# The stored order of a hand-scheduled recurrence and FFN kernel is searched anew

## The chip, the cores and the metric

The kernel runs on one core of one Trainium2 chip. The metric is the device time of one execution in microseconds (us). One core has TensorE (PE, matmuls, with its weight loads shown as PEld), VectorE (DVE), ScalarE (ACT), GpSimd (POOL) and SyncE (SP, which here issues the DMAs). PE writes to PSUM, which has eight banks of 512 fp32 columns on each partition.

## The reference, cut to what matters

```python
def _attn_ref(q, k, v, a_re, a_im):            # (4, 8, 768, 48) each
    mag = np.sqrt(a_re * a_re + a_im * a_im)
    scale = np.minimum(mag, 0.999) / (mag + 1e-06)
    a_re_n, a_im_n = (a_re * scale, a_im * scale)
    S_re, S_im = zeros((B, H, D, D)), zeros((B, H, D, D))
    for t in range(S):
        ar, ai = (a_re_n[:, :, t, :, None], a_im_n[:, :, t, :, None])
        new_re = ar * S_re - ai * S_im
        new_im = ar * S_im + ai * S_re
        kv = np.einsum('bhd,bhe->bhde', k[:, :, t], v[:, :, t])
        S_re, S_im = (new_re + kv, new_im)
        y[:, :, t] = np.einsum('bhd,bhde->bhe', q[:, :, t], S_re)
    return y

def _moe_ref(x, w_in, w_out):                  # (3072, 384), (384, 2048), (2048, 384)
    h = x @ w_in
    g = h * (1.0 / (1.0 + np.exp(-1.702 * h)))
    return g @ w_out

x = attn_out.transpose(0, 2, 1, 3).reshape(3072, 384)
out = _moe_ref(x, w_in, w_out)
```

A gated complex recurrence over 768 steps makes a 48-wide output for each of 4 × 8 heads. The 8 heads of a token stand side by side (384) and go through a two-layer feed-forward block of 2,048 hidden columns. The output of the kernel is written transposed.

## The kernel before, in words

**The recurrence** is computed in chunks. There are 12 units of 256 tokens, three for each batch, and each unit has two chunks of 128 tokens. `prepare(u)` loads the gate values (`ri`) and q and k (`qk`, L406); ACT takes logarithms, exponentials, arc tangents, sines and cosines of them, each of three table sets; DVE forms running sums along the tokens (`tensor_tensor_scan`) and the products that scale and rotate q and k (helper `both`, L276). Five DMAs of SP then move each result from (heads and dims) on partitions into `qkh`, where a head has its own columns (`remap`, L451 to L463). `attend(u)` works on the two chunks: scores on 32-column tiles of the PE array into `p_ps` (L498), times a mask on DVE (`pm`, L502), the mix with v and with the carried state into `x_ps` (L523), a copy to x on ACT (L533) or DVE (L534). For the state, k is turned by PE transposes of 112 × 112, two in one operation, into `k_ps` (L554), copied to `kt` by ACT (L557) or DVE (L558), and multiplied with v on tiles into `z_ps` (L548); DVE adds that to the state (L563, or L567 where the state is new).

**The feed-forward block** `moe(n)` runs for 7 blocks of tokens: units 0 and 1 alone (256 columns, weights and values as whole fp32, one matmul for each product), then five blocks of two units (512 columns, each value split in a high part and a rest, so three matmuls for each product). For each of 8 slices of 256 hidden columns, f = 0 and 1: H (L604) into `h_ps`, the activation G on ACT (L613 whole, L617 split), for the split blocks `gh` (rounded, L620 on ACT or L621 on DVE) and `gl` (the rest, L623 on DVE), then O (L637), which sums all slices into the three `o_ps`. At the end of a block the copies L652 or L653 and one output DMA (three for the last block).

**PSUM.** The eight banks are `p_ps`, `kz_ps` (both `k_ps` and `z_ps` are parts of it), `x_ps`, two `h_ps` and three `o_ps`. With 256 columns the two halves of one `h_ps` bank are used in turn: slice i of half f goes to half i % 2 of `h_ps[f]`.

**Weights** arrive as 64-bit numbers. `convert(n)` rebuilds fp32 from the two words (L294 loads, one of its DVE results is `valA`, L303); `split(n)` makes the rounded part (L312 on ACT, L313 on DVE) and the rest (L315) for the split blocks. `inspect` and `extent` look over all inputs for values outside the fast path's bounds, `decide` counts them, and `general()` would do the work again if any were found. Thirteen matmuls of no consequence (L445) go ahead of the first scores, into `h_ps[0]`.

**The order.** Nothing is issued while it is planned: each of these steps calls `plan.add`, which gives it the next number, the engine that it runs on, perhaps another engine that could do it, and the numbers of the steps that it depends on. Then `Plan.order` reads the stored string: every two bytes are the number of a step, and the steps of `OTHER` change to their second engine.

```python
def order(self):
    coded = base64.b85decode("".join(ORDER))
    order = struct.unpack(f">{len(coded) // 2}H", coded)
    place = {n: i for i, n in enumerate(order)}
    for n in OTHER:
        self.ops[n] = self.alt[n][:2] + self.ops[n][2:3] + self.alt[n][2:] + self.ops[n][4:]
    assert all(place[d] < place[n] for n, o in enumerate(self.ops) for d in o[4])
    return order

with tc.manual_schedule(engines={ENG.PE, ENG.Activation, ENG.DVE, ENG.Pool, ENG.SP}):
    for n in order:
        o = plan.ops[n]
        if o[5] not in (None, cur):
            nc.scalar.preload_act_table_set(o[5])
            cur = o[5]
        o[3]()
```

Each engine runs its own steps in the order of the string. A table of activation functions is loaded (shown at L836) wherever the next ACT step that needs one needs another than the current. What one step must wait for on another engine is enforced by semaphores.

Of the kernel before, what the change touches and what calls it, by code (L numbers as in the profile page):

```python
# [112 lines left out]
}  # L113
ORDER = (
    "08jvb0000A0Ac`<0J#7U08#)^08{`|0D}Nk0E7Ts09F8t0D%Bk0097i09pW800RLE09ybB09gQD0HXk10D=Hz0A>J%01E(L0A~P(0Am1P0EqyH0R"
    "jMN0Ez&J0AT=V0RsSy0R#YQ0Av9L0BZpT0Bit^0S5qW0F(g;0B!(|0B-=50B``00FnT40Sf?-0G0r901yCk0Db^;0GI%E0FwZj0CoVE00sbe00ID"
# [2 lines left out]
    "a<02Kf-0MG!`03-m{02Tlj044y^03`qz0M-E00UrP;0j&WU0NMa20U!X_04@O<05<_4051U>0LB0_0NVh`05AYF05t&00V4o00N?;N06_rZ04V@Q"
    "0Neo{0Nns80NDU50VDw;04xCJ0VM$)06YN80OJ7O0Ve^k0j>ci0Vn|90OA100Vx1N0OSF%0kHuq0ObHf0V)A30kQzh07n4q0kZ%-0WAQ{07L-i05"  # L120
    "||Y0PX-e07U@p06qb^0Qdnf0Pg@g0O$eo0O<fg0O|lq06PJ?0P6w50Pq2{0Pz900kr|Y0mA{f07wD0080Tl0lNVC0Ym{g0gVAV0Wbl?0XqS_0XzX"
    "Q0P+FG0WJZ(0X+de07?P&0Wtx;0P_Jq0mT6`0h<9p0QCXE0W<*g0mlI~0l)zE0YL%t0m=cR0Zjom0m%W&0muMM0Yw4K0XG570YU)x0Zsu%0Qvw;0"
    "Yd@K0Z#!(0Z;+-0aF3b0Z0K!0Q&(^08RnW0ZIT*0ZRe*0rdd<0a5|@0aO7@0Q~|00s8^c0r>%60sH~_0a^i*0+<2*0s#SF0gnOy0sR6A0a*cJ0bv"
    "3L0tx|Z0b2n60s;YC0aXFh0agK50iOY70n`EL0s{gI0o(!v0o4Hi0g(Y_0RRF80oDPj0RaJ*0u2HT0bK!(0tf+K0tW&P0b>FW0uch40uTZc0b~Jf"
    "0o?)>0-6DL0u%w60u}*h0-FLC0cZi<0cio>0gwS$0dWD60-OQS0pbFk0qFsh0pJ3j0uuq(0-pic0-*uf0;U3@0jmLQ0;B=s0qO#!0;2(P0-yq?0;"
    "~by0crxM0hI#l0ptPe0<QsX0dE0x0onnb0dN790doSd0qg;F0p$X*0d@ki0hj`*0owwq0eu0Q0<!|E0wMvN0p<c30p|i30<Hn=0<;0{0iFTx0_*~"
    "<0wV!_0e=E60__4C0eAtR0e}JU0eJ$p0we+(0wn_O0<{7r0eb=*0eS(U0w)5u0ek_X0=NRX0`UQa0r3H)0`CI50w@CX0xtsd0v!VN0v-Y%0=fZ#0"
    "`LO%0=xq90=)t$0fGWB0i*&d0`~$j0xJR_0{H?g0{8)^0yqJK0wDr91BL=J0xbeM0{a3p0fquJ0y_bP0yP3W0yY9Z0{Q`m0j2^!0yhFc0|Ehv0{;"
    "U10!0G-0jL850{#K20f_=c0jvT^0|W+L0g3{@0#5=;1BU`e0gD1h0!so&0!{)`0|f&C0|o|O0|y3Q0!#w{24Dk-0gM9*0|)|80$BqN0#O4A0}lpa"
    "0$2uO1BwF;24e$@0#XAI1C#<y1C9fg0zCtX0#*W40zn330#ycO0?7l724(_X0>A=V0zw1W0>J`T0$T%}0?Gno1B?P(1DXOu24@401D*qt0?Ptm25"  # L130
    "1A21Cs*_0=@=m0?Y%S0@VYN0}KLQ0?z~71C|2K0>T2&0%8Kr1D6A!0>c7d1DFEQ25JJ<0@4GV1DOKE0>uO00@DIy0>%bw0%Zf)25bV~1EB*F0$~D"
    "X0^kFi0>=Vp0@nkh0^tJ40&D}K0%!u_1KI-A1Em7x1E~Vo0^<YS25keX0%`_s0_FnQ25$q~0&W850@?!T1Ed1m0}}(@1E>Pr0&fH10&N541FHk#1"
    "LOi}0^I}U1LFgx0(Js$0~7=20^|m80~`i%0_g+q266)x0&xOs0(b-91Mmar1b+f_1MCCw0)PT}26F@R26O^)26Y4U1M&iM1E&Ia104ev0^S1Z1L*"
    "@E0(Ao)1L_2T1cL+X0}%r#1MUQb10n+;0~Z911c3u70~i8&0~rQ(10e(T0)7K30(%B`10w_N26zI30~!K+0)Ya90~-Q;1NQ?Y0)+!B1cC!41NZ|i"
    "111A31GWRK26+O11GfT%26_W0273eh1cd^M1cn5N1NH=o1GoeF11<x(1d0Rv1FZsv11|=A27Lp%27UuD0*eFv12F`P0*nNV1djrU1dalS12P7G0*"
    "wNW27m;I27v;P0*M5c1jYoA0+Iu}1eXSa12hJM12Y4z2808`0+0ll1d{}j0+9o}1Fr+U1d;@r1HJ;2289E#28IJS28RQ`1Nj3y12qFU0+a(b0+j-"
    "m13d#i133hh13CoA13?6v28aZi28jfe28sha0+$5M1j++H14abL13(1J1jz=A1k3}>28;v11kMAo28{!<1kVGr1k?k=1408t1I+_N1H=TJ1fB!51"
    "4jc$1HlH429E=^29N_q1OEij1#AOJ1knRZ15gB_1kwbZ1k(hg1fK)W15yLU29X2L14{;y16l*d29pC!15E^>1JVP~1l0rp1JeV?29yKH29*QJ1l<"
    "Of1Jnb`15N~_1l|MH1m6Qu15*S62A2ky1mFWt15^f?162f|16%`J16Bi91l9vs1#<;$16c-|178N416>2r2Al-i17rhW1#kmi1Iq<*1mOc>1$qXZ"
    "2A&3=1PKJ<1OfwQ1J(m&17`!*1Qi4W17QZB17ilE18D>P2BHKC1PcV$18)Qj18M}@1lR=J1la>_184<q18WAO1P=zJ1Ox=-2BiaV1O)^J1#bim1#"  # L140
    "|=l1QrAi19$`w2BriT1#$+b1PBFn2B-sU19Jmy2B`+B1$G9j1Q7%p1-}Fm1$P7(1QP@q19=4F1QZ111nC4H1g8UW1Rw^i1R(~k1RDe*19Aqg1RMo"
    ";1S17`1RVtG1$zV~19k&+1SSJ@1Re&j19}Fq19t@I1APXu1SAA21AYU01AGI21SbS61Skfw1T6-$1%n2(1nUEU1TY1J1%(5F1%?Eu2DJn=2DSr&1"
    "TF@*1$+a81h51t1B3;`1gQis1BC=O1$_jj1gZsx1Th3M1;7Tl1TzJG2Dt<(2D$~u1%CyA1m*-Z1UCda2D=152D}722E7D01m^@f1V99(1VIEm1hE"
    "Fb1U&>q2EPS@2EYWo1W5!!1VaVE1hNIf1giwI1WN?01g!?a1hfXi1ib~t2Ezol1U>|}1;ho&1h@o61V;o$1&9Q>2E+!%1WE;g2F3-81<3`=1<D1C"
    "1V{w61<V9a1g->A1g`|X1&Rdr1iu8j1i%DT1osBV1&Id81WyLZ1iJ+61WW|@1W*L+1Wg3N1i}T61j7Z82Fe6c2FnD*1&#*H1Xu)B1jPlB1nvY<1<"
    "eFj1<nLl1YQLB2F(V}1=a@71&st<1X%=H1pEYF1n&f51o{M92G9o41=j}B1p)=n1ZM@)1pNij1p5SB1n>pX1YiVV1=0lm1Y-u%1n~s&2Gj)e1Y`!"
    ")1p@^11=s{-1q1|X1pfqP1Zo6p1oZ~i1ZW1=2G|7*1poyF1q}rO1(O791=<901=R-G1;zw#1qKG%2HOO31r7xV1rG#s1(XKd1Z@Qf2Hgb-1a1c21"
    "at)u1quZc1aJg(1rr2z1rY_?1q%k>1sDe41(gQj1=I!J1bGD-1>XkZ2IB=H1seo+2IK^I1sMkA1snu=1sw+F1tbRN1tSD|1bhU21r!G81(pRB1s("
    "?J1r`M#2I>W!1uO-r1t0|>1tkTZ1ttX-1ug}W1u6w61vUjQ2I~gw1t<pX1uz9I1t|qM2JQtb2JZzi1vdpU1v3TN1)l{w1vCYq2Ji;)1waKk1v&+n"
    "1)~P?1wsX(2J;1~1>6Os1(*fm1(^k!1>*+v1)>Et2K5Eq1bzjp1wID$2KNQv1*HW;1wjR-1w;j#1>pre1xf`y1)K#%2KWZ~1>^-k1xy7?1x5u&2K"  # L150
    "om31+xWD1+E3B1*`?;1xN+01yu!21+)cD1*iu61+@nK1ylvL1-S<P1y%*O2LA=G1-b?21+WFX1+fK51-u6U1-J(R1?UA*1yBX>1-%971@Q%51?mM"
    "+1y==G1y}|01ycp{1z-mP1-=IZ1?2_&1+oS91^or|1?vU%1@{H)1?>e~1^xx@1zH8~1z!bQ1^5MH1_1^61z`pM1^Na61ziUO1!4yU1^Wg91_K3V1"
    "_T9U1!V>W1!o5a2L}cR2M7lV1_lNT1`Gvg2MPua2MY!f1_%Xd1_=fb2Mh)k1!@Kg1#1Tl1{($v1`Y-f1``Gp2Mz}h1{wwy1{Ve&1{ek$1{nq&1|<"
# [857 lines left out]
```

## Time and profile before

| | us |
|---|---|
| time, median of 3 runs | 570.15 |
| time, the runs | 569.31 to 570.60 |
| the profiled execution's own time | 571.31 |
| span of the profiled execution | 569.6 |
| PE busy | 537.4 (94% of the span) |
| DVE busy | 405.6 (71%) |
| ACT busy | 356.5 (63%) |
| POOL busy | 29.1 (5%) |
| table loads of ACT, 77 | 98.8 |
| share of the chain that ended last: PE | 85% |

The TensorE clock was granted in full over the whole span. To read it: busy time is the time in which an engine had an instruction at work; matmuls overlap one another, and their ends are modelled, so the distance between starts tells more of PE than the length of one. A wait is shown with the engine and the line of what ended it.

### The profile page before, as it was taken

How to read it: one execution, taken by the hardware profiler on the slowest of the kernel's cores; microseconds unless marked ns; L12 is line 12 of the kernel's file. 1: busy time of each engine (PE TensorE's matmuls, PEld its weight loads, DVE VectorE, ACT ScalarE, POOL GpSimd, SP SyncE). 2: the span in 40 equal slices, each digit the busy share in tenths (PEclk: the TensorE clock that was granted, in tenths of full speed). 3: DMA queues.
4: the chain of work that ended last, by engine and by line, in shares of the span. 5: the costliest groups of instructions: out<-in, count | busy, mean ns of one | idle time of the engine just before them, and what ended most of it. 6: DMA issues, size and time to landing. Idle time of an engine off the chain costs nothing.

```text
span 569.6 us, 14733 instructions
## 1 busy us (share of the span) xinstructions
PE 537.4 (94%) x6236; PEld 445.9 (78%) x6236; DVE 405.6 (71%) x730; ACT 356.5 (63%) x506; POOL 29.1 (5%) x86
## 2 busy tenths in 40 slices
...
GB/s 341 189 287 342 224 236 133 181 141 144 168 151 207 153 147 177 116 230 138 180 177 82 116 146 230 38 178 163 87 87 18 133 113 58 14 92 10 9 1 67
DMA packets 32341, 81.24 MB, mean 143 GB/s; under 512 B 4368, under 2 KB 8464, under 8 KB 32272
## 3 DMA queue, kind: packets, MB, share of 16 engines
...
q14 instruction: 20, 0.16, 0.1%
...
## 4 chain that ended last, share of the span: by engine, by line
PE 85%; ACT 8%; DVE 3%; issue 2%; DMA 1%; SPq 0%; DVEq 0%; ACTq 0%
PE h_ps L604 34%; PE o_ps L637 34%; PE x_ps L523 6%; PE p_ps L498 5%; PE kz_ps L554 3%; ACT L836 2%; PE kz_ps L548 2%; PE h_ps L445 1%; ACT g L613 1%; DMA qkh<-qr 1%; DMA ri<-in_a_dram 1%; DVE qk L276 1%; ACT s L259 0%; DVE valA L303 0%; DVE qr L276 0%
## 5 line engine op out<-in xcount | busy, mean ns | idle before, releaser
L617 ACT ACTIVATE g<-h_ps 128x512 f32<-128x512 f32 x80 | 46.6, 596 | 96.2 <-PE h_ps L604 69.4
L836 ACT ACT_TABLE_LOAD x77 | 98.8, 1283 | 2.1 <-PEq L999 0.8
L637 PE MATMUL o_ps<-gh,hiU 128*128 128x512 f32 x240 | 96.2, 401 | 0.0
L604 PE MATMUL h_ps<-xhi,hiA 128*128 128x512 f32 x240 | 95.7, 399 | 0.3 <-ACT g L617 0.2
L637 PE MATMUL o_ps<-gl,hiU 128*128 128x512 f32 x240 | 94.0, 392 | 1.4 <-DVE gl L623 1.4
L604 PE MATMUL h_ps<-xhi,loA 128*128 128x512 f32 x240 | 93.7, 391 | 0.0
L637 PE MATMUL o_ps<-gh,loU 128*128 128x512 f32 x240 | 93.5, 390 | 0.0
L604 PE MATMUL h_ps<-xlo,hiA 128*128 128x512 f32 x240 | 93.5, 390 | 0.0
L623 DVE TENSOR_TENSOR gl<-g,gh 128x512 fp32r<-128x512 f32 x80 | 54.3, 686 | 29.7 <-ACT gh L620 27.8
L637 PEld LDWEIGHTS o_ps<-gl,hiU 128*128 128x128 f32 x240 | 45.0, 188 | 11.8 <-DVE gl L623 2.2
L604 PEld LDWEIGHTS h_ps<-xhi,hiA 128*128 128x128 f32 x240 | 45.0, 188 | 10.6 <-ACT g L617 1.1
L637 PEld LDWEIGHTS o_ps<-gh,hiU 128*128 128x128 f32 x240 | 45.1, 188 | 10.0 <-issue 0.8
L604 PEld LDWEIGHTS h_ps<-xhi,loA 128*128 128x128 f32 x240 | 45.1, 188 | 9.6
L604 PEld LDWEIGHTS h_ps<-xlo,hiA 128*128 128x128 f32 x240 | 45.1, 188 | 8.8
L637 PEld LDWEIGHTS o_ps<-gh,loU 128*128 128x128 f32 x240 | 45.1, 188 | 8.6
L621 DVE CAST gh<-g 128x512 fp32r<-128x512 f32 x44 | 18.4, 421 | 45.4 <-PE o_ps L637 44.1
L671 DVE TENSOR_REDUCE fit<-raw_w 128x1 f32<-128x256 f32 x96 | 36.7, 413 | 16.6 <-DMA raw_w<-in_w_out_dram 13.0
L276 DVE TENSOR_TENSOR qk<-qk,s 128x768 f32<-128x768 f32 (+1 forms) x52 | 45.8, 890 | 3.6 <-issue 2.8
L604 PE MATMUL h_ps<-x,valA 128*128 128x256 f32 x192 | 46.3, 386 | 1.9 <-ACT g L613 1.2
L557 ACT ACTIVATE kt<-kz_ps 128x224 f32<-128x224 f32 x59 | 20.7, 351 | 41.4 <-PE kz_ps L554 26.9
L637 PE MATMUL o_ps<-g,valU 128*128 128x256 f32 x192 | 45.2, 384 | 0.8 <-ACT g L613 0.8
L502 DVE TENSOR_TENSOR pm<-p_ps,mask 128x512 f32<-128x512 f32 x48 | 32.8, 684 | 15.1 <-PE p_ps L498 14.0
...
## 6 DMA issues: line engine op xcount, KB each, us to landing
...
```

Source lines behind the costliest of these rows:

```text
L276: add(en, t, rank, lambda: e.tensor_tensor(out=out, in0=a, in1=b, op=alu), **kw)
L498: mm(p_ps[to : to + QL, j, lo:L], lhsT=at(h, 1, c)[:, lo : lo + QL], rhs=at(h, 0, c)[:, lo:L], start=True, stop=True)
L502: add("DVE", d_t(CW), rk(4 * c + hh), lambda hh=hh: dve.tensor_tensor(out=pm[hh], in0=p_ps, in1=mask, op=ALU.mult), r=["P"], w=[f"pm{hh}"])
L523: mm(x_ps[32 * j : 32 * j + 32, r, :], lhsT=lt, rhs=rt, start=n == 0, stop=n == len(steps) - 1)
L557: one = ("ACT", a_t(2 * KD) - 0.12, lambda e=e: act(out=kt[0][:, 2 * e : 2 * e + 2, :], in_=k_ps, func=AF.Copy))
L604: mm(h_ps[hb][:, hs], lhsT=ww[:, r * T + f * P : r * T + (f + 1) * P], rhs=x[:, r, :], start=r + k == 0, stop=r == NR - 1 and k == len(ter ...
L617: add("ACT", a_t(N) - 0.15, rk(i + f / 2), lambda hb=hb, hs=hs: act(out=g32[hb][:, hs], in_=h_ps[hb][:, hs], func=AF.Silu, scale=SLOPE), r ...
L621: two = ("DVE", d_t(N, 2), lambda hb=hb, hs=hs: dve.tensor_copy(out=high.g(hb)[:, hs], in_=g32[hb][:, hs]))
L623: add("DVE", d_t(N), rk(i + f / 2), lambda hb=hb, hs=hs: dve.tensor_tensor(out=glo[hb][:, hs], in0=g32[hb][:, hs], in1=high.g(hb)[:, hs].b ...
L637: mm(o_ps[m][:, 0:N], lhsT=y[:, f * DM + m * P : f * DM + (m + 1) * P], rhs=x[:, hs], start=i == 0 and f == 0 and k == 0, stop=i == NP - 1 ...
L671: add("DVE", d_t(CK), rk + 2, lambda x=x, op=op: dve.tensor_reduce(out=f_w[:, x, n : n + 1], in_=weights.looked_at()[:, :, 1], op=op, axis ...
L836: nc.scalar.preload_act_table_set(o[5])
```

## The change

`OTHER`, the set of steps that run on their second engine, goes from 113 numbers to 128: 46 leave and 61 join. `ORDER` becomes another order of the same 1,817 steps. Nothing else changes: the same steps, tiles, buffers and matmuls. The string is not readable by itself; its beginning stands here, and the prediction says what it decodes to.

```diff
 CLEAR = 513
 OTHER = {
-    102, 105, 152, 254, 256, 319, 332, 340, 393, 394, 399, 401, 403, 407, 411, 415, 421, 427, 431, 451,
-    499, 500, 522, 566, 583, 586, 593, 596, 603, 613, 633, 653, 661, 666, 688, 691, 738, 744, 749, 771,
...
+    102, 105, 152, 203, 254, 256, 336, 340, 393, 394, 395, 397, 403, 407, 409, 411, 415, 419, 423, 425,
+    431, 500, 525, 547, 571, 583, 593, 596, 603, 606, 623, 633, 646, 653, 660, 661, 662, 666, 688, 691,
...
 }
 ORDER = (
-    "08jvb0000A0Ac`<0J#7U08#)^08{`|0D}Nk0E7Ts09F8t0D%Bk0097i09pW800RLE09ybB09gQD0HXk10D=Hz0A>J%01E(L0A~P(0Am1P0EqyH0R"
...
+    "08jvb015yA0Ac`<00jUK0HXj=08#){08;>g09F8109OE90Du5m09XKm01E(F09ybJ0A2uH0A&D$0A>JR0097l0Am1#0A~PT0B8V-0E7Tx0Av7)0E"
...
 )
```

Decoded, the new order differs from the old one in 407 of PE's 479 steps; ACT has 436 steps instead of 429, DVE 661 instead of 668, and POOL and SP have 72 and 169 in both. The kinds of steps that change engine are `gh` (11 from ACT to DVE, 20 back), the copies to `kt` (20 from ACT to DVE, 15 back), copies of x (5 each way), copies of the output (5 from DVE to ACT), rounded weights (5 from ACT to DVE, 4 back) and 17 small steps of `prepare`. Table loads are 70 instead of 77.

## Rows read from the trace of the kernel before

**Rows 1.** Busy time by stretch: stretch, us, then PE, PEld, DVE, ACT, POOL, clock, DMA

```profile
0.00:20.00 20.00, 0.00 (x0) 0.00 (x0) 15.82 (x38) 17.03 (x28) 9.54 (x27) 1.00 0.86 329
40.00:240.00 200.00, 194.65 (x2598) 162.51 (x2597) 184.11 (x295) 176.12 (x246) 13.87 (x35) 1.00 0.70 183
240.00:560.00 320.00, 320.00 (x3291) 266.14 (x3290) 184.25 (x357) 144.21 (x206) 3.89 (x18) 1.00 0.40 104
560.00:569.60 9.60, 4.96 (x22) 3.38 (x21) 2.96 (x10) 1.20 (x2) 0.00 (x0) 1.00 0.23 85
```

**Rows 2.** What PE waited for, 40 to 569 us: us in total, times, longest

```profile
PE o_ps L637 <- DVE gl L623: 1.4, 1, 1.4
PE h_ps L604 <- ACT g L613: 1.2, 2, 0.7
PE kz_ps L548 <- ACT kt L557: 0.9, 2, 0.5
PE o_ps L637 <- ACT g L613: 0.8, 2, 0.5
PE kz_ps L554 <- DVE st L563: 0.5, 1, 0.5
PE h_ps L604 <- DVE valA L303: 0.4, 1, 0.4
PE h_ps L604 <- ACT x L533: 0.3, 1, 0.3
```

**Rows 3.** PE's timeline around transposes: start, us, line, tile, shapes, count, [idle before, releaser]

```profile
81.24 0.41 PE L554 MATMUL kz_ps<-ident,qkh 112*128 112x112 f32 x2 [0.45 <-DVE st L563]
81.58 0.31 PE L498 MATMUL p_ps<-qkh 128*32 128x128 f32 x3
...
182.69 0.35 PE L554 MATMUL kz_ps<-ident,qkh 112*128 112x112 f32 x2
182.82 0.48 PE L637 MATMUL o_ps<-gh,hiU 128*128 128x512 f32 x1
183.13 0.39 PE L637 MATMUL o_ps<-gh,loU 128*128 128x512 f32 x1
183.36 0.40 PE L637 MATMUL o_ps<-gl,hiU 128*128 128x512 f32 x1
...
184.99 0.36 PE L554 MATMUL kz_ps<-ident,qkh 112*128 112x112 f32 x2
185.27 0.24 PE L548 MATMUL kz_ps<-v,kt 128*32 128x48 f32 x2
...
208.29 0.50 PE L637 MATMUL o_ps<-gh,hiU 128*128 128x512 f32 x1
208.63 0.39 PE L637 MATMUL o_ps<-gh,loU 128*128 128x512 f32 x1
...
471.67 0.41 PE L554 MATMUL kz_ps<-ident,qkh 112*128 112x112 f32 x2
471.85 0.48 PE L637 MATMUL o_ps<-gh,hiU 128*128 128x512 f32 x1
...
493.11 0.39 PE L637 MATMUL o_ps<-gl,hiU 128*128 128x512 f32 x1
493.43 0.31 PE L523 MATMUL x_ps<-pm,v 128*32 128x128 f32 x3
```

**Rows 4.** Timeline of SP and of DVE around unit 7's load of q and k

```profile
210.65 0.61 SPq L406 DMA_DIRECT2D qk<-in_qk_dram  x1
...
221.56 0.96 DVE L276 TENSOR_TENSOR qk<-qk,s 128x768 f32<-128x768 f32 x1 [2.76 <-issue]
```

**Rows 5.** Costliest groups: line, operation, count, then busy us, mean ns, idle before

```profile
L836 ACT ACT_TABLE_LOAD x77 | 98.8, 1283 | 2.1 <-PEq L999 0.8
```

**Rows 6.** Timeline of SP and PE at unit 0: last remap's issue, second chunk's scores

```profile
29.59 0.60 SPq L463 DMA_DIRECT2D qkh<-qk  x1
...
33.84 0.32 PE L498 MATMUL p_ps<-qkh 128*32 128x128 f32 x4
```

More of the change, by code (lines that the diff above doesn't have):

```diff
@@ L106 @@
 OTHER = {
[6 rows of a table removed]
[7 rows of a table added]
 }
 ORDER = (
-    "08jvb0000A0Ac`<0J#7U08#)^08{`|0D}Nk0E7Ts09F8t0D%Bk0097i09pW800RLE09ybB09gQD0HXk10D=Hz0A>J%01E(L0A~P(0Am1P0EqyH0R"
-    "jMN0Ez&J0AT=V0RsSy0R#YQ0Av9L0BZpT0Bit^0S5qW0F(g;0B!(|0B-=50B``00FnT40Sf?-0G0r901yCk0Db^;0GI%E0FwZj0CoVE00sbe00ID"
-    "<0C)hK0C@nN0Ga>@0D1ri0G<GQ0H6ST0G|L10HFa101^NZ00{uB0Hgq|01W_r0So}80HOd60H^@20Hy&A0S*AC0IvZM022VR0I2{O0I&fM00aOY0"
-    "IC490I>lP02BbU0Tuwd03!gk0UQAm0TckX0Kx#f0ILBL0Tlql0Ji|V0Js3e0KEXd0T%%n0KWjh0L1{v02%<n0M7s%02=@w0384z0L}m*04)I303r"
@@ L119 @@
[L119 to L153, printed above, removed]
@@ L154 @@
-    "d{1|9|>1|$X|1||k01}6q71}+9F2M`7;2N4D+1}_FI1~UdQ1~>*W1~LXM208{d1~djW20{io1~&#h20I2k215o!20jKq20#W!222J;20;c*21o`*"
-    "2NDKO21y4K21*7?22Tc222ci422%$V22=+X2Nnia23H1J22}=G23!Xh23Q9e23r"
+    "08jvb015yA0Ac`<00jUK0HXj=08#){08;>g09F8109OE90Du5m09XKm01E(F09ybJ0A2uH0A&D$0A>JR0097l0Am1#0A~PT0B8V-0E7Tx0Av7)0E"
+    "YmJ0Ehts0BHdV0F40y0J#AK0BQjR0BZnj0R{k!0Br#W0F(f30FD4}0F?l60FMBc0C51200sdF0CE7B0Db_I0GR-D01yBN0FnT70Gt2}0Gj}H0G$B"
+    "|0G9v=00IDZ0G<E|0CxbI0C)il00RJ@0Hgq*0IUF|0C@nR0S*8X0HOe>0Hy#A0IdNG0ImS10D1tg0Sy2V0I&di0I>lO0DJ%w02u&%03HDk0I~oC0"
@@ new lines @@
+    "I2|~0J8xR0Tuuh0JH$Q03!gk0TckM0UQ9f0TKYa0Kx$k0Ji|V0TTeY0K)*p0KEXd0T=+k0T%$k0L1{v02%<n0Mq~+02=@w03iS%0M!5;0L}m+04)"
+    "F&0M`IA0LB0$0MGyy0M7sy044y*03`qz0MY=~0UrP;0MP)-0j&Vj0T}=%0N4Q_04@MG0U7|{0U-b{0UH1_0NDUA0V4o405kwG0NMa406_rT05$;J"
+    "04o4007d}b0UiL|0VDw;04xCC0VM$)06YP&0O0{A0OA3z0VV+`0PFzc0LK9-05|~c0V@Hq0V)A30OkNW073z>0OtTi06G9e0WAPM0OSF=06zfb0O"
+    "$Zm06qXk0O|ng0Pg@h0PX=V0P6ri0rCLL0lEN50P_K`0m1;x0Qmv407wAv0L=lk07?PB0P+E~0k;7}0WJVb0gnN;0k{D;0lNV(0mA_J0XYFN0lWb"
+    "^0mK0^0XqS`0W<-P0XzZ40lon70X+dT0rLR#0X_l70QLdF0Y3r90l)!30W|?Z0QCVj0m=aS0muPD0m%W&0XG3f0rUY)0n7nL0QUh-0Q&$;0Yd@K0"
@@ new lines @@
+    "Y?E(0rmk%0Z9SR0Z;*z0ZIYQ0ZRe*0rdgU0Z{==0aF410r&x50geIt0a^i60sH_?0r~(<0a*dk0r>%708at|0h<9;0jU7|0to>90bv1K0g(az0c8"
+    "PF0R9300tNy70agJ20bBx@0s;aG0o(ys0i6NU0cHUJ0ayV60gwUc0c!!&0s{fj0t*3M0t5lw0u2HM0bT+O0tW&P0b>FP0uKTZ0p0;;0o4Iw0ucdd"
+    "0b~Ld0uljf0-ORA0u}+^0g?h20-XVI0;U0K0iyz^0oDO*0-pk!0+|7m0uur00jC150pJ1G0oVa;0oeg_0-FM`0dE1H0d4}Z0dNAW0ht1x0-ynP0-"
+    "*un0_y?l0e1qT0<r?60h9ru0;2+@0pbC80onqn0pkJW0qX(f0;vJ!0qg;C0vG|70;&SD0ha-N0;>V%0owwu0wMwJ0dxWG0<8kH0q+5N0=EHq0vQ7"
+    "B0xkiA0=5FU0_*}B0=WXU0fYkX0e=D`0e%6P0`UQw0d@lK0=oh50we;u0viJG0=xlx0i^+)0=)ty0r3L#0ek_T0`&qM0w@9<0`~$Y0xtoe0{8;<0"
@@ new lines @@
+    "v-Y%0fqu60f7Q30x$v~0fhqd0xAMA0{a3h0e}K50fGV{0{jC10fz!D0x|->0{sD^0jmNt0{#N|0yF|O0i*)J0yYBj0f+)O1BL;n0!0G)0|Ej#0z?"
+    "8y0f_;q0g3`S0|No70#5=)0|Wv`0|f&H0jvT#0!{&o0!jv50y_dr0!RW=0|5gE0z3jf0!#wI0zU(Y0}2BO23`XI0#E`#0!;&l244dS0#OEF0gM7c"
+    "0}cXM1Bn9<0}BI+0}TU=0?7hd24Mzb1CIhd24e$`0#pMK1CRnz0zv}91B(Jf1Cat%0#*Xb1Cj=01Cs`20=@!W0#^oR0>c7Y1C#<=1C0X90%HQq1C"
+    "|0_1K0w@0$&4_1DXQX0?h-R0>uKx1D68N0$c)O1DFP92517%1DOM!25AEf1D^uX0$>7U1E2%n1EB-p1EK<K0@ng(0>=W*25JJ;0@4Cy1K9%D0%ii"
+    "!25SOt1Dpci25bUh0^kD@0>}f}0@(wj1DgVN1KR_o1KtAR0%`-P1EvDv1K|d31F8e!25ts#0_6g40}}(|0@MSf0@?!O0^0+q0_FnT1Ka{|0_Or~0"
@@ new lines @@
+    "&N1_1FHkw0^R~?0^|b}0&4^20&xa#1LOj90&)ZA1LX#B1Ly{F0_X&P0(Sy)0(b-O0(k=!0(%4O0_g^G0~`W%1MmYK0_p~I0}%#w1Mvgt1E&KX0)P"
+    "V_1cw9a0~Q2>1M32O10n)}0(u051M>up1b_qb1MUMC10VzK11SR-26h610~rG&26qI826zJ`0)7K110@8G0(}I510e${0)GO70)zyD1N8!h0*C_|"
+    "1M~)Y26_V<273ed111A21NH=k1NZ~10*VC211toH1N#Jt11AQ211$oE1d0Rv27LoA1NsJj11|!H1FZs#1N{Rq1GWN<0*eHe12F=L0*?fj1GfZ=27"
+    "d&M27m)H0*(fO1egSm0+ItX27&`K1j+`31Fi;y1ds%i0+0mD0+9o_13Uzg1Gxmv1d;^K0+Rzb289I228ITQ1H1!012_Vd12qDb12zJd1k?jQ0+$0"
+    "i28afU1eFGg1Nj7+1G)pT133e)1e*kz14aX|1HA;C13?Ch1jqxj1G57^1H%Kf1HJ=01HT501GNT?13&}91jz%;14si$1G@u4149JN1H=PF295;J2"
```

18 lines of the change are left out of this document (added), and 9 rows, old and new, of the table OTHER.

## The prediction

> **What bounds the kernel now.** First read the busy time by stretch [rows 1]. PE does nothing in the first 20.00 us, has work in 194.65 of the 200.00 us from 40 to 240, and in all of the 320.00 us from 240 to 560; in the last 9.60 it works 4.96. No work is added or removed on PE, so a new order can only win where PE waits or where one matmul follows another late. From 40 on, waits are 200.00 − 194.65 = 5.35 us. In the same stretch DVE works 184.11 and ACT 176.12 of 200.00, so both are close behind PE; after 240 ACT is down to 144.21 of 320.00, and neither limits anything.
>
> Then read what PE waited for between 40 and 569 us [rows 2]. Four of the seven rows are of one kind. A matmul into h_ps or o_ps waits 1.2 and 0.8 us, two times each, for the ACT silu L613 of a whole block; z (L548) waits 0.9 us, two times, for the copy kt L557; transposes (L554) wait 0.5 us once for the state add L563. In each of these one PSUM bank changes hands: the two halves of h_ps[f] share a bank, and k_ps and z_ps are two parts of kz_ps. That is 3.4 us in 7 waits. The other rows (gl 1.4, valA 0.4, x 0.3) are waits for data.
>
> These views understate a wait. PE's ends are modelled: a matmul of 512 columns is shown as 0.39 long while the next starts 0.23 behind it (183.13 to 183.36) [rows 3]. So each wait costs PE 0.39 − 0.23 = 0.16 more than the idle time shown.
>
> **The change, part by part.** Both strings can be decoded by hand: each pair of bytes is the number of an operation. All 1,817 operations stay, and OTHER moves some to their second engine. Places and counts below are from that decoding.
>
> *Bank hand-overs, the gain.* Before, a whole-block H or O stands with almost no PE work between the last matmul into a bank and the first that needs its reader: in the three tightest places 0.00, 0.00 and 0.13 us of matmuls (at the pace of 0.23). After, the tightest place has 0.96. I take it that the four silu waits and the one state-add wait go. z stands directly behind its transposes in 6 places before, and in 3 after, so half of its cost stays. Gain: (3.4 + 7 × 0.16) − (0.9 + 2 × 0.16) / 2 = 4.5 − 0.6 = 3.9 us. The bounds are 0 (each wait is replaced by one of its size) and 4.5. I take 3.9, since the distance of 0.96 exceeds the longest of these waits, 0.7 [rows 2].
>
> *Transposes moved, a small gain.* The 80 pairs of transposes (L554) stand in four kinds of places, whose price I read in the stretch around each [rows 3]:
> - alone between two big matmuls: 182.69 to 183.13 is 0.44, against 0.23 for one pair of big matmuls without it: 0.21.
> - between a big matmul and tiled work (which uses 32 columns of the array): 0.28 to the tiled start (184.99 to 185.27). Without it the tiled work starts 0.32 after the big matmul (493.11 to 493.43), 0.09 over the pace. Price 0.28 − 0.09 = 0.19.
> - between tiled work and a big matmul: 0.18 (471.67 to 471.85), and the next gap is 0.31 (182.82 to 183.13), 0.08 over the pace; without it that gap is 0.34 (208.29 to 208.63), 0.11 over. Price 0.18 + 0.08 − 0.11 = 0.15.
> - between tiled work: 0.34 (81.24 to 81.58).
>
> Before: 14, 47, 12 and 7 pairs, or 2.94 + 8.93 + 1.80 + 2.38 = 16.05 us. After: 35, 14, 27 and 4, or 7.35 + 2.66 + 4.05 + 1.36 = 15.42. I take −0.6. Bounds: −2.3, if a lone pair costs only its own 0.13 (182.69 to 182.82; 0.08 less for each of the 21 more), and +4.4, if the 21 are paid for at 0.21 and the pairs beside tiled work were free.
>
> The Trainium skill ("TensorEngine Tiling (Array Packing)", section "Key Properties") says that changing the tiling mode drains TensorE. The entry of 0.32 and the return of 0.34 agree with it. By this rule only the switches between full and tiled work would count, which are 117 before and 116 after; the term would be 0 instead of −0.6, and the time 566.6.
>
> *A new tight place.* The first H of block 1 stands close behind the copy L533 of unit 1, with 0.58 us of PE work between; a row of that kind is 0.3 [rows 2]. I take +0.3; bounds 0 and +0.6.
>
> *Data waits left alone.* The one long wait, gl 1.4, comes from unit 7's qk load: SP issues it at 210.65, and DVE, idle for 2.76, goes on at 221.56 [rows 4]. That is 10.9 us of transfer and queue. In the new string the load stands about as far ahead of its first user as in the old one (6.0 us of PE work against 6.2), though gl of the MoE block now stands ahead of the waiting DVE operation. I take 0, since DVE is held for as long in either order; bounds −1.5 (1.4 + 0.16 goes) and +0.7. The first uses of weight slots A7, A6 and U7 are 5.8, 2.6 and 1.4 us of PE work behind their readiness (2.6, 8.2 and 1.4 before): 0.
>
> *Table loads.* 77 become 70, at 1.283 us each [rows 5]: 9.0 us of ACT. They are hidden, since ACT was idle for 24 of the 200 us from 40 to 240 and more later [rows 1]. I take 0.
>
> *Engine moves.* OTHER gives 31 gh, 35 kt, 15 x and out copies, 9 weight splits and 17 preparation operations to the other engine; ACT ends with 7 more, DVE with 7 fewer. At the longest DVE operation quoted, 0.96 us [rows 4], seven add at most 6.7 us to ACT, less than the 9.0 that its table loads give back. Cover gone would mean a wait at a silu; the no-change rival has that.
>
> *Start and end.* Unit 0's remaps are issued on SP until 30.2 (29.59 + 0.60), and the scores of its second chunk start at 33.84 [rows 6]; five of 13 warm matmuls now stand inside chunk 0 instead of one. No remap moves earlier, so 0, bounds ±0.7. The last PE work ends 4.6 us before the end of the span (9.60 − 4.96) [rows 1]; the last output transfer comes behind it in both orders. 0.
>
> **Sum.** −3.9 − 0.6 + 0.3 = −4.2. The profiled execution (571.31, span 569.6) would be 567.1. The median of the runs shown, 570.15, lies 1.16 under the profiled one; I subtract from the median: 570.15 − 4.2 = 566.0 us.
>
> **The rivals.**
> *More gain.* The searched order could also remove the data waits, as it was given other durations: gl 1.4, valA 0.4 and x 0.3, with 0.16 each: 2.6 more, or 563.4. For it: gl now precedes the waiting DVE operation. Against it: the load of unit 7 is as late as before. Chance 0.10.
>
> *The waits only move.* DVE at 184.11 and ACT at 176.12 of 200.00 leave 16 and 24 us [rows 1]. If they, not the bank order, hold PE back from 40 to 240, then a wait taken away at one silu comes back at the next copy or gl. The time stays at 570.2. For it: three of the seven wait rows are for data that DVE or ACT made late. Against it: PE waits for nothing from 240 on, where banks change hands just as often. Chance 0.22.
>
> *Slower: transposes at the head of PE's queue.* The new order puts 35 pairs alone among big matmuls; each needs kz_ps to be free, so the copy kt or state add of the pair or z before it must be over. PE runs in order: all matmuls behind the pair wait too. Such a wait cost 0.45 + 0.16 = 0.61 at 81.24 [rows 3]. It decides once it comes in 9 of the 80 places or more: 566.0 + 9 × 0.61 = 571.5. With 14 of them the time is 566.0 + 8.5 = 574.5. For it: pairs placed straight behind another pair's copy rise from 39 to 52. Against it: pairs straight behind a state add fall from 30 to 11. Chance 0.18.
>
> That the change doesn't do what it says has no place here: both strings hold the same numbers, and the new places are seen in them.
>
> **How the numbers follow.** A measurement here can tell 0.2% from no change, 1.14 us: faster is below 569.0, slower above 571.3. The forecast has 0.50, with its own range from 563.7 (the bound of −2.3 in place of −0.6, and the z waits gone as well, 0.6) to 569.0. With more gain, faster gets 0.60; the moved waits are the 0.22 of no change; slower has 0.18. The range from 562.8 to 573.0 leaves out the low end of the second case and more than half of the slow one, some 0.15.
>
> **What would show it.** In the new trace, waits of h_ps and o_ps for L613 should be gone, those of z for L557 at 0.4 us or less; the sum of PE's waits from 40 to 240 near 2.7 us instead of 5.35; table loads 70; lone transposes at 0.44 to the second matmul after. If transposes wait for L557 or L563 in nine places or more, the slow rival was right. If PE's idle time is unchanged but other engines are named, the waits moved. If PE waits less and the span is no shorter, the price of the transposes was wrong.

## The result and the profile after

The kernel after takes 563.94 us (median of 4 runs, 563.29 to 565.69) against 570.1 before: ratio 0.9898, 95% interval 0.9872 to 0.9924. That is 6.2 us less by the medians and 5.8 by the ratio (the ratio on record is not quite the quotient of the medians, here and below). The forecast was 566.0, range 562.8 to 573.0: the direction was right and the size too small by 2.1 us. In the profiled executions the span fell from 569.6 to 562.7, by 6.9 us. The profiled execution of before (571.31) was slower than all four timed ones (569.31 to 570.60), so the waits in its trace may lie above those of a usual execution.

First the busy time by stretch of the kernel after, with the columns of [rows 1]:

```profile
0.00:20.00 20.00, 0.04 (x1) 0.07 (x1) 15.97 (x38) 17.13 (x29) 8.59 (x26) 1.00 0.87 327
40.00:240.00 200.00, 199.09 (x2596) 167.77 (x2595) 189.07 (x306) 180.34 (x251) 10.83 (x35) 1.00 0.72 191
240.00:560.00 320.00, 317.48 (x3310) 259.93 (x3308) 179.07 (x347) 134.76 (x202) 3.79 (x18) 1.00 0.39 101
```

From 40 to 240 PE is now idle for 0.91 us instead of 5.35. DVE (189.07) and ACT (180.34) are busier there than before (184.11 and 176.12), so neither was at its limit, taken in sum. Below 320 in the last row only says that PE is done at 557.48.

Next what PE waited for in the kernel after, 40 to 569 us, the view of [rows 2]:

```profile
PE h_ps L605 <- DVE valA L304: 0.6, 1, 0.6
PE p_ps L499 <- DVE pm L503: 0.3, 1, 0.3
```

All seven waits that the prediction counts as bank hand-overs are gone, and so is the long one for gl (lines are one higher in this kernel: L605 is L604 of before). So is a wait that [rows 2] leaves out, the eighth row of that view of before:

```profile
PE h_ps L604 <- ACT g L617: 0.2, 1, 0.2
```

Then the first H of block 0, the point at which the feed-forward work starts, in PE's timeline before:

```profile
39.65 0.48 PE L604 MATMUL h_ps<-x,valA 128*128 128x256 f32 x1 [0.29 <-ACT x L533]
```

and after:

```profile
38.75 0.48 PE L605 MATMUL h_ps<-x,valA 128*128 128x256 f32 x1 [0.29 <-ACT x L534]
```

It comes 0.90 earlier. (Its wait for x is the row of 0.3 in [rows 2]; it is still there.) Adding up the 6.9 us: 0.90 at the start. Behind the first H, PE's timeline shows 10 waits of 5.26 us before and 2 of 0.91 after; with 0.16 more for each wait, as the prediction had it, 5.63. PE needs 518.73 instead of 525.33 from there to its last end (564.98, now 557.48), or 6.60; what the waits don't explain is 0.97. The rest behind PE's end takes 0.60 more (562.7 − 557.48 = 5.22 against 4.62). 0.90 + 5.63 + 0.97 − 0.60 = 6.90.

The table loads are 70, as decoded:

```profile
L837 ACT ACT_TABLE_LOAD x70 | 89.8, 1283 | 2.0 <-PEq L1000 0.8
```

### The profile page after: what moved, and what is told of

It is laid out like the page before. It is cut to its first block, busy times and chain, and to the rows that moved or that the text cites. A ratio compares the mean times of both kernels' runs of the same rounds, so it can differ in the third digit from the quotient of the medians.

```text
span 562.7 us, 14718 instructions
## 1 busy us (share of the span) xinstructions
PE 535.0 (95%) x6236; PEld 442.2 (79%) x6236; DVE 403.4 (72%) x723; ACT 351.1 (62%) x506; POOL 25.8 (5%) x86
## 4 chain that ended last, share of the span: by engine, by line
PE 85%; ACT 5%; DMA 4%; DVE 3%; issue 1%; POOL 0%; DVEq 0%
PE o_ps L638 35%; PE h_ps L605 33%; PE x_ps L524 7%; PE p_ps L499 5%; PE kz_ps L555 3%; PE kz_ps L549 2%; DMA raw<-in_w_in_dram 2%; DMA ri<-in_a_dram 1%; ACT L837 1%; DMA raw<-in_w_out_dram 1%; ACT s L260 1%; DVE qk L277 1%; DVE valA L304 0%; ACT s L374 0%; DVE qr L277 0%
## 5 line engine op out<-in xcount | busy, mean ns | idle before, releaser
L605 PE MATMUL h_ps<-xhi,hiA 128*128 128x512 f32 x240 | 97.0, 404 | 0.0
L605 PE MATMUL h_ps<-xhi,loA 128*128 128x512 f32 x240 | 93.9, 391 | 0.0
L605 PE MATMUL h_ps<-xlo,hiA 128*128 128x512 f32 x240 | 93.6, 390 | 0.0
L605 PEld LDWEIGHTS h_ps<-xhi,loA 128*128 128x128 f32 x240 | 45.0, 188 | 9.8
L605 PEld LDWEIGHTS h_ps<-xhi,hiA 128*128 128x128 f32 x240 | 45.1, 188 | 8.9 <-issue 0.2
L605 PEld LDWEIGHTS h_ps<-xlo,hiA 128*128 128x128 f32 x240 | 45.2, 188 | 8.5
L558 ACT ACTIVATE kt<-kz_ps 128x224 f32<-128x224 f32 x54 | 19.0, 352 | 48.9 <-PE kz_ps L555 21.1
L621 ACT ACTIVATE gh<-g 128x512 fp32r<-128x512 f32 x45 | 28.0, 628 | 31.4 <-PE o_ps L638 31.1
L605 PE MATMUL h_ps<-x,valA 128*128 128x256 f32 x192 | 45.3, 384 | 0.9 <-DVE valA L304 0.6
L622 DVE CAST gh<-g 128x512 fp32r<-128x512 f32 x35 | 14.7, 423 | 36.7 <-PE o_ps L638 30.6
```

Source lines behind the costliest of these rows:

```text
L558: one = ("ACT", a_t(2 * KD) - 0.12, lambda e=e: act(out=kt[0][:, 2 * e : 2 * e + 2, :], in_=k_ps, func=AF.Copy))
L605: mm(h_ps[hb][:, hs], lhsT=ww[:, r * T + f * P : r * T + (f + 1) * P], rhs=x[:, r, :], start=r + k == 0, stop=r == NR - 1 and k == len(ter ...
L621: one = ("ACT", a_t(N) - 0.1, lambda hb=hb, hs=hs: act(out=high.g(hb)[:, hs], in_=g32[hb][:, hs], func=AF.Copy))
```

## The experiments

All kernels differ from before or after in the order, in the engines or in table loads, and compute the same; names with b_ start from before, with a_ from after, and line numbers in the rows differ from kernel to kernel by some lines. Single steps are moved by a few lines in `Plan.order`, shown here with the moves of one experiment:

```diff
+MOVES = (
+    (634, 1006),
+)
...
+        order = list(order)
+        for n, ahead_of in MOVES:
+            order.remove(n)
+            order.insert(order.index(ahead_of), n)
         place = {n: i for i, n in enumerate(order)}
```

The kernel before ran beside each set, with medians of 570.33, 570.38 and 570.66 us. Where an order is put together from two, the lines of Python show how the stored string was made.

### The bank waits alone (b_bank)

```diff
+MOVES = ((212, 207), (213, 207), (207, 36), (215, 209), (209, 37),  # 44.55
+         (232, 239), (57, 64), (62, 64), (248, 240),                # 71.06 and valA
+         (305, 318), (363, 343),                                    # 81.24; 102.04, 104.87
+         (359, 666), (360, 666), (377, 750), (496, 750))            # 116.23; 140.90
```

There are 15 moves, not the 13 of the text below.

> The kernel before, with 13 steps moved in its order so that the seven PE waits for the other engine's access to a PSUM bank (0.75, 0.47, 0.45, 0.47, 0.39, 0.28 and 0.49 us in the trace of before) and the one for valA (0.41) have PE work in front of them. No engine is changed and nothing else is moved. If the waits are made by the order of the accesses to a bank: 3.3 + 0.41 + 8 x 0.16 = 5.0 us less, 565.1 us, and none of these waits in the trace. If DVE and ACT hold PE back from 40 to 240 us, the waits come back under other names and the time stays at 570.1.

568.46 us, ratio 0.9954 (0.9926 to 0.9983): 2.6 us less by the ratio (1.0 to 4.2), 1.9 by the medians. What PE waited for, 40 to 569 us:

```profile
PE kz_ps L575 <- ACT kt L578: 1.1, 1, 1.1
PE h_ps L625 <- ACT x L554: 0.3, 1, 0.3
PE p_ps L519 <- DVE pm L523: 0.2, 1, 0.2
```

Every wait that was aimed at is gone, gl's too, which was not touched. One of 1.08 came up in another place: transposes at 77.48 wait for a copy kt. ACT starts this copy at 77.10, 0.30 earlier than before, behind a conversion of a weight, but PE is there 1.4 us earlier than before (at 76.40 instead of 77.85). From the first H to PE's last end the profiled execution took 520.02 us instead of 525.33, 5.3 less, as expected. The timed gain is smaller, and the expected 5.0 lies outside its interval: the profiled execution (566.59) is one of the fastest of 12 (566.33 to 570.87), and that of before took longer than its timed runs, so the difference between the two traces is an upper end. That waits only move falls as an account of the whole: of 5.26 us of waits behind the first H 1.26 are left, and the time went down. In part it holds, for the 1.08.

### The long wait for gl alone (b_gl)

The move is the one shown above: 634 (gl) ahead of 1006 (the product with unit 7's k).

> The kernel before, with one step moved: gl of block 2, slice 5, f 0, ahead of the DVE product that waits for unit 7's load of q and k. If the long wait of PE for gl was made by the place of gl behind a DVE step that waits for a transfer: 1.35 + 0.16 = 1.5 us less, 568.6, with DVE still held for as long. If it matters only that DVE is held (the reason for which the prediction took 0), the wait passes to the next DVE result, the mask product or the state add: 570.1.

570.06 us, ratio 0.9993 (0.9963 to 1.0023): not told apart from no change. In DVE's timeline gl now runs ahead of the product:

```profile
218.11 0.68 DVE L630 TENSOR_TENSOR gl<-g,gh 128x512 fp32r<-128x512 f32 x1
219.60 0.96 DVE L283 TENSOR_TENSOR qk<-qk,s 128x768 f32<-128x768 f32 x1 [0.81 <-ACT s L380]
```

The wait for gl is gone from PE. The next H, with its wait for ACT, is what is late behind it, 0.51 instead of 0.20:

```profile
224.20 0.50 PE L611 MATMUL h_ps<-xhi,hiA 128*128 128x512 f32 x1 [0.51 <-ACT g L624]
```

So in this trace the wait went with the place of gl, and its price was no more than 1.35 + 0.16 − 0.31 = 1.2 us; the timing allows a gain of 2.1 us and a loss of 1.3. DVE was not held for as long as before either (0.81, not 2.76), though only gl had been moved, so one trace does not separate the two. The wait itself also differs between traces in which gl stands where it did: it is 1.35 in before, 0.63 in b_start and 0.42 in b_lone, so 1.35 is the longest of the three.

### The start alone (b_start)

```python
first = new_order[:168]
order = first + [n for n in old_order if n not in first]
```

> The first 168 steps (to the copy of x that the first H waits for) in the new order, all others in the old one; the two sets of 168 steps are the same, and none of them changes engine. If the two waits of transposes on the kz_ps bank in chunk 0 (0.68 and 0.69 us) set the start of the first H: 0.9 us less, 569.2, the first H at 38.75 instead of 39.65. If SP's issue of the remaps sets it, as the prediction had it: 570.1.

568.76 us, ratio 0.9969 (0.9940 to 0.9997): 1.8 us less (0.2 to 3.4), and the 0.9 lies in that range. The first H comes at 38.83, and transposes no longer wait in chunk 0; SP issues the same remaps as before and none earlier (the last at 29.76 instead of 29.59). But in the profiled execution another wait grew from 0.41 to 1.62, for a weight slot, and took back more than the start had won:

```profile
69.44 0.45 PE L603 MATMUL h_ps<-x,valA 128*128 128x256 f32 x1 [1.62 <-DVE valA L302]
```

That execution took 571.24 us, 2.5 more than the median of its kernel, so its longer wait is not shown to be the rule: the median has a gain. What the trace shows is that the start's 0.9 can be lost again where the weights are not ready.

### The three together (b_all)

The new start as above, and the 15 moves and 634 ahead of 1006.

> The three edits together: the new start, the 13 moved steps and the moved gl; all engines and all other places as before, so the transposes stand as before and there are 77 table loads. If the waits account for the change: 5.0 + 1.5 + 0.9 = 7.4 us less, 562.7, as fast as the new order or faster by up to 1.2 us. If the moved transposes, the engines or the table loads had a part in it, it stays above 563.9 by that part; if waits move, above 567.

566.44 us, ratio 0.9914 (0.9879 to 0.9949): 4.9 us less than before by the ratio (2.9 to 6.9), 3.9 by the medians. The three ratios multiplied give 0.9916: the parts add up, though not to the 7.4 expected from the traces. With the old engines, 77 table loads and the old places of the transposes behind the start this is most of the change (5.8 by the ratio, 6.2 by the medians). From the first H to its last end PE takes 521.30 us here and 518.73 in the kernel after, 2.57 more. Some 1.6 of that are waits, 40 to 569 us:

```profile
PE kz_ps L553 <- ACT kt L556: 1.1, 1, 1.1
PE h_ps L603 <- ACT g L616: 1.1, 1, 1.1
PE p_ps L497 <- DVE pm L501: 0.2, 1, 0.2
```

Two waits of 1.1 have come in where others left; the other 1.0 is not in waits that the profile shows. The moves by hand cleared the places that were seen; the searched order has none of these.

### Transposes alone between big matmuls (b_lone)

28 moves, each a pair of transposes ahead of the big matmul operation before it, as

```diff
+    (341, 363), (482, 369), (484, 362), (546, 381), (548, 376), (552, 388),
...
```

> The kernel before with 28 pairs of transposes, which stood between a big matmul operation and tiled work, each moved ahead of that operation, so that they stand alone between big matmuls as 35 pairs of the new order do (42 alone instead of 14). By the prediction's prices, 0.21 alone against 0.19 there: +0.6 us, 570.9. By its upper bound, every lone pair paid for in full: +5.9, 576.2. By the slower rival, a lone pair at the head of PE's queue waits 0.45 + 0.16 for the copy or state add ahead of it on kz_ps: +0.6 for each that waits, seen in the trace by name.

572.02 us, ratio 1.0036 (1.0021 to 1.0050): 2.0 us more (1.2 to 2.9), or 0.07 for a pair. The prices of the prediction gave 0.02. PE's timeline agrees with the 0.07: where a pair went from one stretch to the next, the first gets shorter by 2.0 to 2.1 us, a big matmul operation and the pair, and the next longer by some 0.06 more than that, at most of the moves. One of the 28 places has a wait at the head of the queue, and it shows what the slower rival meant:

```profile
225.28 0.42 PE L588 MATMUL kz_ps<-ident,qkh 112*128 112x112 f32 x2 [0.48 <-ACT kt L591]
```

One is not nine: that rival falls, and so does the bound of 0.21 for each pair. In the kernel after a lone pair costs what the prediction read, 0.44 from its start to the second matmul behind it, less 0.23:

```profile
183.86 0.36 PE L555 MATMUL kz_ps<-ident,qkh 112*128 112x112 f32 x2
183.98 0.48 PE L638 MATMUL o_ps<-gh,hiU 128*128 128x512 f32 x1
184.30 0.39 PE L638 MATMUL o_ps<-gh,loU 128*128 128x512 f32 x1
```

### Seven table loads put back (a_tables)

```diff
+TWICE = (279, 442, 513, 679, 762, 917, 999)
...
         if o[5] not in (None, cur):
+            if n in TWICE:
+                nc.scalar.preload_act_table_set(min({LOGS, TRIG, SILU} - {cur, o[5]}))
             nc.scalar.preload_act_table_set(o[5])
```

> The kernel after with one more table load ahead of the arc tangent of units 1 to 7: 77 loads as before instead of 70, 9.0 us more of ACT before 240 us. If the seven loads fewer cost and gain nothing, because ACT has idle time there: 563.9. If ACT holds PE back in that stretch: up to 572.9, with PE waits for ACT results.

567.70 us, ratio 0.9957 (0.9942 to 0.9971), 3.8 us more than after's 563.94 (3.4 by the two ratios). What PE waited for, 40 to 569 us:

```profile
PE h_ps L606 <- ACT g L615: 0.9, 1, 0.9
PE h_ps L606 <- DVE valA L305: 0.7, 1, 0.7
PE p_ps L500 <- DVE pm L504: 0.7, 1, 0.7
PE kz_ps L556 <- ACT kt L559: 0.4, 1, 0.4
PE o_ps L639 <- ACT g L615: 0.3, 1, 0.3
```

Three of the five are ACT's: g, kt, g. ACT had 20 us idle from 40 to 240 (200 − 180.34), and six more loads there, 7.7 us, still made PE wait 3.03 us in the stretch instead of 0.91. The seventh stands ahead of the first H, which comes at 39.53 instead of 38.75, 0.78 of the 3.8:

```profile
35.42 1.28 ACT L839 ACT_TABLE_LOAD   x1
39.15 0.41 PE L556 MATMUL kz_ps<-ident,qkh 112*128 112x112 f32 x2 [0.96 <-ACT kt L559]
```

So idle time of ACT in sum was not cover; the loads delay the step behind them, and that step was wanted. In the change itself this does not come up: by the ACT timelines 46 loads have started by 240 us before and 47 after, 8 of them ahead of 40 us in both, and behind 240 us PE waits for nothing in either. The seven loads fewer lie where no wait could be saved.

### Order and engines taken apart (b_other, a_other)

The old order with the new `OTHER`, and the new order with the old one.

> The order of before with the engines of after: the 107 steps that change engine do so, nothing else. If the engines alone made a part of the gain: below 570.1 by that part. If they only fit the order that they were searched with: steps come late where an engine's queue grows, PE waits more than the 7.4 us of before, 570.1 to 573.

576.58 us, ratio 1.0124 (1.0092 to 1.0155): 6.2 us more than before by the medians, 7.1 by the ratio.

> The order of after with the engines of before. If the gain lies in the order alone: 563.9. If the engines have a part: above that by it; the bank hand-overs that the new order keeps clear would be tight again where the reader is on the other engine, 565 to 568.

569.29 us, ratio 0.9985 (0.9969 to 1.0002): not told apart from before, so nearly all of the gain is lost. What PE waited for in the new order with the old engines, 40 to 569 us:

```profile
PE o_ps L636 <- ACT g L612: 1.5, 3, 0.8
PE p_ps L497 <- DVE pm L501: 1.4, 1, 1.4
PE x_ps L522 <- DVE st L562: 0.6, 1, 0.6
PE kz_ps L553 <- ACT kt L556: 0.5, 1, 0.5
```

The silus of whole blocks are waited for again, three times, and the mask product for 1.4. Neither half of the change is shown to be a gain without the other. That does not make the new engines necessary: the three edits above got 4.9 us with the old ones.

### The second half, a step put back, two more steps moved (a_again, a_early, a_gl, a_best)

The last four ran together, beside the unchanged kernel after.

> The kernel after, unchanged, on the chip and in the same rounds as the next three, so that they can be held against it: ratio to before 0.990 as in the result, some 564.4 beside 570.3.

563.76 us, ratio 0.9879 (0.9843 to 0.9914). Its trace has waits of 1.05 us behind the first matmul instead of 2.49: those for the mask product at 27.8 (1.01 in the first trace, 0.15 in this) and for a weight (0.57, none here) change from execution to execution.

```python
first = new_order[:969]        # engines of these as after, of the others as before
order = first + [n for n in old_order if n not in first]
```

> The new order and engines for the first 969 steps (to the last O of block 2, near 240 us), the old order and engines for the rest; table loads 47 up to the cut as after, 27 behind it as before. If the gain is made up to 240 us, where the waits were: the same as the kernel after within 0.3 us, which is what the transposes behind the cut cost more (7.38 against 7.04 us by the prices). If the second half has a part in it: above after by that part.

568.45 us, ratio 0.9968 (0.9941 to 0.9994), 4.7 us over a_again. Not as either reading had it: the seam makes waits of its own, of which one is the longest behind the first matmul in any run,

```profile
249.40 0.80 PE L603 MATMUL h_ps<-xhi,hiA 128*128 128x512 f32 x1 [2.04 <-ACT g L616]
```

and one of 0.53 at 245.91. Of the 4.28 us by which PE ends later (561.32 against 557.04), waits account for 3.87 − 1.05 + 0.16 = 2.98. The other 1.3 are covered by the clock of TensorE. Behind the two waits the profile shows it granted at 0.50, the lower of its two levels (1.2 and 2.4 GHz), in the columns of [rows 1]:

```profile
249.40:252.56 3.16, 3.16 (x8) 2.48 (x9) 3.16 (x6) 1.81 (x4) 0.00 (x0) 0.50 1.01 243
252.56:256.00 3.44, 3.44 (x16) 2.83 (x15) 3.28 (x7) 2.30 (x4) 0.00 (x0) 1.00 0.60 80
```

and the matmuls of 512 columns start 0.43 apart there instead of 0.23:

```profile
250.42 0.63 PE L603 MATMUL h_ps<-xhi,loA 128*128 128x512 f32 x1
250.85 0.63 PE L603 MATMUL h_ps<-xhi,hiA 128*128 128x512 f32 x1
```

In the 4.00 us up to 249.40 PE had worked 1.45. From 249.40 the seven gaps between starts take 3.16 us instead of 1.61, so the slow clock cost some 1.5. Its waits and the clock behind them thus cover the whole loss in the trace, and the second half is not shown to have a part in it.

```diff
+MOVES = (
+    (634, 809),
+)
```

> The kernel after with gl of block 2, slice 5, f 0 put behind the two DVE products of unit 7's q and k again, where the old order had it. If its place ahead of them is what took the long wait away: PE waits for gl again, up to 1.5 us more than after. If the earlier load (issued at 206.95, with the product at 215.29 not waiting) and the later O (its first gl matmul at 219.21) are enough, gl ends near 217.8 and nothing changes.

564.09 us, ratio 0.9897 (0.9857 to 0.9936): not told apart from a_again. PE has no wait at all from 40 us on in its trace. In the kernel after, DVE did not wait for unit 7's load, issued at 206.95:

```profile
206.95 0.61 SPq L407 DMA_DIRECT2D qk<-in_qk_dram  x1
```

```profile
215.23 0.16 DVE L432 TENSOR_SCALAR small<-s 128x3 f32<-128x3 f32 x1
215.29 0.95 DVE L277 TENSOR_TENSOR qk<-qk,s 128x768 f32<-128x768 f32 x1
```

The product starts right behind the step ahead of it. The load took less time, as the view of DMA issues shows (KB each and us to landing), in the kernel after:

```profile
qk<-in_qk_dram SPq DMA_DIRECT2D x1, 768.0 KB, 4.8
```

and in the kernel before:

```profile
qk<-in_qk_dram SPq DMA_DIRECT2D x1, 768.0 KB, 10.8
```

Against [rows 4] that is the difference: no hold, so no late gl, wherever gl stands. It goes with the order: this load takes 8.5 to 10.8 us in the seven traces that have the old order there, and 4.8 to 5.1 in the seven that have the new one, with the old engines (a_other) too.

```diff
+MOVES = (
+    (159, 161),
+    (160, 161),
+    (59, 69),
+)
```

> The kernel after with three steps moved: the first mask product (DVE) ahead of two rotations of unit 0, which takes the wait of 1.01 at 27.78, and the conversion of weight slot A6 ahead of that of A7, which takes the wait of 0.57 at 69.05. If the waits are all that is left before 240 us: up to 1.01 + 0.57 + 2 x 0.16 = 1.9 us less than after, 562.5. If unit 0's remaps set the start behind the first wait and the weight transfers the second: no change.

564.81 us, ratio 0.9889 (0.9853 to 0.9925): no gain. The wait for the mask product went, and the remaps, which depend on the two rotations put behind it, came late instead:

```profile
33.95 0.31 PE L564 MATMUL kz_ps<-ident,qkh 112*128 112x112 f32 x1 [0.44 <-DMA qkh<-qk]
...
40.16 0.48 PE L614 MATMUL h_ps<-x,valA 128*128 128x256 f32 x1 [0.29 <-ACT x L543]
```

The first H is at 40.16, 1.34 later than in a_again (38.82). With the rotations moved behind the mask product the remaps bind the start; in the old order the kz_ps waits came first. None of these kernels is shown to be faster than after.

### All kernels in one table

For each profiled execution: the waits of PE's timeline behind its first matmul, and the time from the start of that matmul to PE's last end, less the waits and 0.16 for each of them. The last column is the same rest counted from the first H.

| kernel | first matmul to last end | waits (number) | the rest | from the first H |
|---|---|---|---|---|
| before | 544.91 | 7.39 (15) | 535.1 | 518.5 |
| after | 537.52 | 2.49 (5) | 534.2 | 517.5 |
| a_again | 537.02 | 1.05 (4) | 535.3 | 517.7 |
| a_gl | 536.45 | 1.41 (3) | 534.6 | 517.7 |
| a_best | 538.46 | 1.45 (5) | 536.2 | 517.9 |
| b_bank | 540.37 | 3.40 (7) | 535.9 | 518.4 |
| b_all | 540.08 | 3.36 (6) | 535.8 | 518.5 |
| a_tables | 541.20 | 4.45 (8) | 535.5 | 517.9 |
| a_early | 541.29 | 3.87 (5) | 536.6 | 519.6 |
| a_other | 541.90 | 5.10 (9) | 535.4 | 518.2 |
| b_gl | 543.13 | 5.95 (13) | 535.1 | 518.4 |
| b_start | 544.73 | 6.34 (12) | 536.5 | 518.5 |
| b_lone | 545.25 | 6.55 (14) | 536.5 | 519.8 |
| b_other | 550.40 | 10.28 (20) | 536.9 | 519.8 |

The first column spans 14 us, the rest 2.7 and the rest from the first H 2.3. So most of what these kernels differ by is waits of PE. A wait ahead of the first H does not count in full, since PE can lose the time again at the next one: after waits 1.01 for the mask product at 27.78 and a_again 0.15, and their first H comes at 38.75 and 38.82. That is why the last column is the steadier one: 518.4 to 518.5 in the five traces with the old order or nearly (before, b_bank, b_gl, b_start, b_all), 517.5 to 517.9 in the five with the new order and engines (after, a_again, a_gl, a_best, a_tables). The new order thus has some 0.7 less between the waits, and not only by the luck of one execution. That this is the transposes' −0.6 is not shown: b_other has the matmuls in the order of before and a rest 1.3 above it.

## Why the prediction came out right, and where it was too small

**Bank hand-overs.** Forecast −3.9; in the trace all seven are gone, 3.3 + 7 × 0.16 = 4.4. The half of the z waits that was kept (0.6) did not appear. The moves alone (b_bank) take the waits away with the old engines, so they were made by the order and not by full engines; timed, they give 2.6 us (1.0 to 4.2), less than the 5.0 read from the trace of before. That all seven are hand-overs of a bank is too much said: z multiplies kt, the very copy that it waits for, so those two (0.9) are waits for data as well. The two of O are for g, which O reads, but at 71.06 that g was late because its silu had waited for a matmul into the other half of the bank:

```profile
70.62 0.66 ACT L613 ACTIVATE g<-h_ps 128x256 f32<-128x256 f32 x2 [0.80 <-PE h_ps L604]
```

**Long wait for gl: the step that failed.** "I take 0, since DVE is held for as long in either order." DVE was not held at all: the product with unit 7's k waited 0 instead of 2.76, because the load landed in 4.8 us instead of 10.8 (the product starts 8.34 us behind the issue; before, without the hold, it would have been 8.15). In the two traces that is −1.35 − 0.16 = −1.5, the bound that was given; timed, b_gl shows no gain (2.1 less to 1.3 more). I had counted the PE work between the load and its user, which was the same; the transfer's own time was not in that count. b_gl shows that the wait can be taken away by gl's place too, a_gl that the new order did not need it.

**The start: the other step that failed.** "No remap moves earlier, so 0". Measured −0.9. No remap did move earlier, but the remaps did not bind the old start (their issue runs to 30.8, not 30.2: the last row of [rows 6] is one issue of two): two transposes waited 0.68 and 0.69 for kz_ps between 31 and 34 us. My waits began at 40 us, so these two of the same kind were left out. b_start gets the 0.9, and a_best shows the remaps binding once those waits are gone and the remaps come late.

**The end.** Taken as 0; what follows PE's last end takes 0.60 longer. In the traces, then, the 2.7 us between the 6.9 measured and the 4.2 forecast are gl 1.5, the start 0.9, the bank waits 0.5, the tight place 0.3 and smaller ones 0.1, less the end's 0.6. So the forecast came as near as it did in part because a miss at the end made up for others.

**The tight place at block 1.** Forecast +0.3; no wait there (the row of 0.3 that it was priced by is the first H of block 0, part of the start). Smaller ones came elsewhere, in this trace: valA 0.57 instead of 0.41, and pm 0.34.

**Transposes.** −0.6 against a rest of 0.97 that has more in it. The price of a lone pair reads the same in the new trace (0.44 − 0.23 = 0.21), but in b_lone a pair moved costs 0.07 and not 0.02: the term rests on differences of a few hundredths, and one of them was wrong. With 0.05 more for each of the 21 more lone pairs it would be some +0.4 instead of −0.6, an estimate. So the gain that was forecast from the transposes is not shown.

The Trainium skill ("TensorEngine Tiling (Array Packing)", section "Key Properties") says that changing the tiling mode drains TensorE. If such changes were all that matters, as the prediction worked out from it, a lone pair would cost no more than one beside tiled work. b_lone does not bear that out: 2.0 us (1.2 to 2.9) for 28 pairs.

**Table loads and engines at 0.** The reason was wrong: idle time in sum did not cover 9.0 us of loads in a_tables (3.8 us), nor the engine moves in either direction (5.4 us in a_other, 6.2 in b_other, by the medians). For the loads the value 0 is still likely, since none was saved ahead of 240 us. For the engines it is not settled: b_all, with the old loads and engines, is slower than after by 0.9 us by the two ratios (0.9914 and 0.9898) and by 2.5 by the medians, and its interval alone reaches from 1.1 faster to 2.9 slower.

**The rivals.** "More gain" gave 563.4, half a microsecond from the result, but that is luck for the most part: of its three data waits only gl's went, and by a faster load; valA's grew from 0.41 to 0.57, and that for x is still 0.29 at the first H. "The waits only move" is refuted for the change (5.35 us idle became 0.91), though b_bank and b_all show one and two waits of 1.1 that came up in other places. The slower rival has no wait of transposes at all in the new trace behind 40 us. On the signs named ahead: PE's idle time fell below the 2.7 forecast, the loads are 70, lone pairs cost 0.44.

**Open:** where the 0.97 (some 0.7 over ten traces) that the waits don't explain comes from: the places of the transposes, the order of the other steps on PE, or waits too short to show.
